# Gathering six of the last eight mode rows before the last weights are in, in a fused linear-attention and spectral-mixing kernel

## The chip, the cores and the metric

One Trainium2 chip, and of its cores one. The metric is the device time of one execution in microseconds (us). Before the change it is 421.44 us, the median of three runs that lie between 421.43 and 421.51.

## The reference

Eight batches, eight heads, 576 positions, head size 64, so 512 channels. A linear attention with the feature map phi(x) = elu(x) + 1 gives x; a real Fourier transform along the positions keeps 64 modes; each mode multiplies its own complex 512 x 512 weight; the inverse transform gives y, and a channel product with a ReLU closes it.

```
kv = einsum('bhsd,bhse->bhde', phi(k), v);  num = einsum('bhsd,bhde->bhse', phi(q), kv)
x  = num / (den + 1e-06)                    # rearranged to (8, 576, 512)
X  = rfft(x, axis=1)[:, :64]
Yr = Xr @ w_r - Xi @ w_i;   Yi = Xr @ w_i + Xi @ w_r        # per mode, 512 x 512 each
u  = x + irfft(Yr + 1j * Yi, n=576, axis=1)
out = u + maximum(u @ w_ch, 0.0)
```

The weights of the 64 modes are 128 MB in float32, by far the most of what is read.

## The kernel before

**Order of the work.** First comes the attention and the forward transform, while inputs and the first weights arrive. Then a loop over 32 pairs of modes (`mode_pair`, lines 462 to 483): each pair's 2 MB of weights (in bf16) come by two transfers on the GpSimd queue (POOL), TensorE (PE) multiplies them, and small transposing products (`picks`) put the mode rows, 16 columns for each mode (real and imaginary part of eight batches), into a PSUM tile `yt_ps`. Between the pairs, work on earlier modes is dealt out from a list (`work_slot`). PE is given filler products (`keep_warm`, line 416), as many as the table `FILL` of line 535 says for the pair. `pin` keeps an instruction in program order on its engine.

**The last pair** is mode 62 and mode 63 (`last_pair`, lines 487 to 519). Their weights come as eight transfers (`w_load_last`, line 122): three of 512 KB, and the fourth cut into five pieces, three of 128 KB and two of 64 KB (`PIECES`), so that PE can follow each piece as it arrives (line 513). The rows of the last eight modes (56 to 63) are gathered in `Y8`: modes 56 to 62 at line 506, mode 63 at line 519.

**The late rows.** With `Y8` complete, lines 921 to 950 turn it: four transposes give the rows y (128 rows, 8 modes x 16), eight products of 128 x 256 with the channel weights give z, the same rows after the channel product. Both go into one tile `last` of 128 partitions x 2 x 512 (f16). Two transfers, one on the SyncE queue (SP) and one on POOL (lines 946 to 950, 256 KB each), then spread these rows into `YZ_all`, which holds for every batch and each of two halves of the partitions the 64 rows of modes 32 to 63: every fourth row is one of the last eight modes.

**The end.** The output is 36 tiles of 128 positions x 512, taken as 18 pairs. For each pair, `channels` (line 792) puts the channel product's early part into a PSUM accumulator, `add_inverse(n, 1)` (line 755) adds the part from z, a ReLU on ScalarE (ACT) follows, `add_inverse(n, 0)` adds the part from y, and VectorE (DVE) adds x; then SP stores. Batches 0 and 1, which are pairs 0 to 3, read `last` directly with 128 rows (`lead_sb`); all others read `YZ_all` with 64 rows (`inv2_sb`), tile 0 of a pair from partitions 0 to 63 and tile 1 from 64 to 127. For pairs 0 to 3 the order is written out by hand, tile by tile (lines 982 to 988): for each of seven tiles, in turn, PE adds the y part, makes the sums of one tile two pairs ahead (`sums_of`: channels, z part, ReLU), and DVE adds and SP stores 256 KB (`add_one`, line 960). The sums ahead are those of pairs 2, 3 and 4, a tile at a time. From pair 5 on whole pairs are handled (`rectified`, `finish`, lines 806 and 829), with one DVE addition of 128 x 1024 and one store of 512 KB.

```
    singles = [(n, i) for n in range(4) for i in range(2)][1:]
    ahead = [(n, i) for n in (2, 3, 4) for i in range(2)]
    for n, i in singles:
        add_inverse(n, 0, (i,))
        if ahead:
            sums_of(*ahead.pop(0))
        add_one(n, i)
```

The functions that the change touches:

Of the kernel before, what the change touches and what calls it, by code (L numbers as in the profile page):

```python
# [10 lines left out]
F32 = mybir.dt.float32  # L11
F16 = mybir.dt.float16
# [31 lines left out]
def kernel(  # L44
# [10 lines left out]
    nc = tc.nc  # L55

    B, H, S, Dh = q.shape
    D = H * Dh
    NM = moe_w_r.shape[0]
    NHP = H // 2  # L60
    NDC = D // 128
# [5 lines left out]
    NL = 8  # L67
    NE = NM - NL
    NF = NM // 2

    fwd_np, inv_np, pick_np = _dft_consts(S, NM)
    id16_dr = nc.inline_tensor(np.eye(128, dtype=np.float16), name="ident16")
# [8 lines left out]
    id16 = const.tile([128, 128], F16, name="id16")  # L81
    fwd_sb = const.tile([128, 5, 2 * NM], F16, name="fwd_sb")
    pick_sb = const.tile([128, 32], F16, name="pick_sb")
    wch16 = const.tile([128, NDC, D], F16, name="wch16")
# [21 lines left out]
    pin = tc.keep_in_program_order  # L106
# [15 lines left out]
    def w_load_last(pool, tag: str, bufs: int):  # L122
        w_in[LAST] = pool.tile([128, NDW, D], BF16, tag=tag, bufs=bufs, name=f"w{LAST}")
        for g in range(2):
            for half in range(2):
                rows_in = (moe_w_r, moe_w_i)[half][NM - 2 + g].rearrange("(p dc) e -> p dc e", dc=NDL)
                for dcs in PIECES if (g, half) == (1, 1) else (slice(0, NDL),):
                    dst = w_in[LAST][half::2, g * NDL + dcs.start : g * NDL + dcs.stop]
                    pin(nc.gpsimd.dma_start(out=dst, in_=rows_in[:, dcs, :]))

    w_in: dict[int, object] = {}


    W_PRE = 3
# [16 lines left out]
    def rows_of(jj: int, base: int = 0):  # L151

        if jj < NJJ:
            return slice(base + jj, base + 512, NJJ)
        return slice(512, S) if base == 0 else slice(0, base)
# [268 lines left out]
    def work_slot(p: int, name: str):  # L424
        for _ in range(slots.get((p, name), 0)):
            if work:
                work.pop(0)()
# [59 lines left out]
    def last_pair():  # L487
        xl = ystage.tile([128, NDL, 2 * B], BF16, name="xl")
        for h in range(2):
            src = xt_v[:, (2 * h + 1) * NDC : (2 * h + 2) * NDC, :, :, LAST]  # L490
            pin(
                nc.vector.tensor_copy(
                    out=xl[:, h * NDC : h * NDC + NDC], in_=src.rearrange("p c t b -> p c (t b)")
                )
            )
        w = w_get(LAST)
        kk = NM - 2
        work_slot(LAST, "start")
        P = psW.tile([128, D], F32, tag="P", bufs=2, name=f"P{kk}")
        for dc in range(NDL):  # L500
            n = 32 if dc < NDC else 2 * B
            product(P, xt_cols(dc, kk, n), n, w, dc, NDL)
        st = evacuate(kk, P)
        work_slot(LAST, "mid")
        picks(kk, st, 1)
        pin(nc.vector.tensor_copy(out=Y8[:, :, 0 : NL - 1, :], in_=yt_ps[:, :, 0 : NL - 1, :]))
        keep_warm(3)
        y_last = psW.tile([128, NDC, 2 * B], F32, tag="P", bufs=2, name="y_last")
        for piece in PIECES:
            for dc in range(piece.start, piece.stop):  # L510
                for ec in range(NDC):
                    pin(
                        nc.tensor.matmul(
                            y_last[:, ec, :], w[:, NDL + dc, ec * 128 : ec * 128 + 128], xl[:, dc, :],
                            start=(dc == 0 and ec == 0), stop=(dc == NDL - 1), skip_group_check=True,
                        )
                    )
            keep_warm(WARM[piece.stop])
        nc.vector.tensor_copy(out=Y8[:, :, NL - 1, :], in_=y_last)

# [9 lines left out]
    psW = tc.alloc_tile_pool(name="psW", bufs=1, space=PSUM, side="left")  # L530
# [1 line left out]


    n_early = n_keep + n_pre
    FILL = {**{p: 7 for p in range(5, 16)}, **{p: 7 for p in range(18, 27)}, 27: 7, 28: 10, 29: 12, 30: 10}
    ystage = ctx.enter_context(tc.tile_pool(name="ystage", bufs=1, side="right"))
    inv_sb = ystage.tile([2 * NM, S], F16, name="inv_sb")
    inv2_sb = ystage.tile([128, S], F16, name="inv2_sb")
# [1 line left out]
    lead_sb = [ystage.tile([128, S], F16, name=f"lead{b}_sb") for b in range(N_LEAD)]  # L540
    nc.sync.dma_start(out=inv_sb, in_=inv_dr.ap())
    YE_T = ystage.tile([128, NDC, NF, 2 * B], F16, name="YE_T")
    YL = [ystage.tile([128, NDC // 2, 2, 2 * NL, NF // NL, B], F16, name="YL0")]
    Y8 = ystage.tile([128, NDC, NL, 2 * B], F16, name="Y8")

    def late_modes(g: int, ps):

# [19 lines left out]
    yt_ps = None  # L567
# [9 lines left out]
    sW = ctx.enter_context(tc.tile_pool(name="sW", bufs=1))  # L577
# [4 lines left out]
    YZ_all = sW.tile([128, B, 2, D], F16, tag="YZ", bufs=1, name="YZ_all")  # L582
# [24 lines left out]
    last_ps = []  # L607
# [67 lines left out]
    x16w, xTw = {}, {}  # L675
# [79 lines left out]
    def add_inverse(n: int, half: int, tiles_of=(0, 1)):  # L755

        def mm(i, orow, l, r):
            on_bank(
                n, {i},
                nc.tensor.matmul(  # L760
                    accs[n][orow, i], l, r, start=False, stop=True, skip_group_check=True
                ),
            )

        for i in tiles_of:
            for b, jj, orow in parts_of(pairs[n][i]):
                sel_rows = rows_of(jj, BASE[b % 2])
                if n < 2 * N_LEAD:
                    mm(i, orow, lead_sb[b][:, sel_rows], last[:, half, :])
                else:  # L770
                    g = HALVES[i]
                    mm(i, orow, inv2_sb[g, sel_rows], YZ[b][g, half, :])
# [19 lines left out]
    def channels(n: int, tiles_of=(0, 1)):  # L792
        if n not in accs:
            accs[n] = acc_pools[n % 4 // 2].tile([128, 2, D], F32, tag="acc", bufs=2, name=f"acc{n}")
        for i in tiles_of:
            t = pairs[n][i]
            for cols, src in e0_parts(t):
                on_bank(
                    n, {i},
                    nc.tensor.matmul(  # L800
                        accs[n][:, i, cols], id16, src, start=(cols.start == 0), stop=False,
                        skip_group_check=True,
                    ),
                )
# [103 lines left out]
    for p in range(n_early, LAST):  # L908
        mode_pair(p)
    assert not work  # L910
    psB.release()
    acc_pools.append(
        tc.alloc_tile_pool(name="psT0", bufs=1, space=PSUM, side="right", reuse_waits="tile")
# [2 lines left out]
    for n in range(N_PRE):  # L916
# [1 line left out]
    last_pair()  # L918


    last = sW.tile([128, 2, D], F16, tag="rows", bufs=1, name="last")
    z1_ps = psW.tile([128, NDC, 8, 2 * B], F32, tag="yt", bufs=1, name="z1l")
    y_ps = [
        psW.tile([128, NDC, 128], F16, tag="P", bufs=2, name=f"ypl{h}")[:, 0 : NDC // 2] for h in range(2)
    ]
    y0 = psW.tile([128, D], F32, tag="P", bufs=2, name="y0l")
    last_ps.append(z1_ps.rearrange("p c m n -> p (c m n)"))
    rows = [Y8[:, ec].rearrange("p m n -> p (m n)") for ec in range(NDC)]
    hw = D // 2
    COLS = [slice(h * hw, h * hw + hw) for h in range(2)]  # L930
    for ec in range(NDC):
        pin(nc.tensor.transpose(y_ps[ec // 2][:, ec % 2, :], rows[ec], id16))
    pin(nc.scalar.copy(out=last[:, 0, COLS[0]], in_=y_ps[0].rearrange("p c r -> p (c r)")))
    pin(nc.vector.tensor_copy(out=last[:, 0, COLS[1]], in_=y_ps[1].rearrange("p c r -> p (c r)")))
    for h in range(2):
        for ec in range(NDC):
            pin(
                nc.tensor.matmul(
                    last_ps[h][:, 0:hw], rows[ec], wch16[:, ec, COLS[h]],
                    start=(ec == 0), stop=(ec == NDC - 1),  # L940
                )
            )
        pin(nc.scalar.copy(out=last[:, 1, COLS[h]], in_=last_ps[h][:, 0:hw]))
    pin(nc.tensor.matmul(y0, lead_sb[0][:, rows_of(0)], last[:, 0, :]))
    pin(nc.vector.tensor_tensor(out=x_of(0), in0=y0, in1=x_of(0), op=ALU.add))
    for h, eng in enumerate((nc.sync, nc.gpsimd)):
        eng.dma_start(
            out=YZ_all[64 * h : 64 * h + 64 : NF // NL].rearrange("r b z d -> r b (z d)"),
            in_=last.rearrange("p z d -> p (z d)"),
        )  # L950
    psW.release()
    acc_pools.append(
        tc.alloc_tile_pool(name="psT1", bufs=1, space=PSUM, side="left", reuse_waits="tile")
# [2 lines left out]
    def relu(n: int, i: int):  # L956
        a = accs[n][:, i]
        on_bank(n, {i}, nc.scalar.activation(out=a, in_=a, func=AF.Relu))
# [3 lines left out]
        on_bank(n, {i}, nc.vector.tensor_tensor(out=x_of(t), in0=accs[n][:, i], in1=x_of(t), op=ALU.add))  # L962
        store(t, 1)

    def sums_of(n: int, i: int):
        channels(n, (i,))
        add_inverse(n, 1, (i,))
        relu(n, i)

    add_inverse(0, 1, (1, 0))  # L970
    on_bank(
# [2 lines left out]
            out=x_of(0), in0=accs[0][:, 0], scalar=0.0, in1=x_of(0), op0=ALU.max, op1=ALU.add  # L974
# [5 lines left out]
        add_inverse(1, 1, (i,))  # L980
        relu(1, i)
    singles = [(n, i) for n in range(4) for i in range(2)][1:]
    ahead = [(n, i) for n in (2, 3, 4) for i in range(2)]
    for n, i in singles:
        add_inverse(n, 0, (i,))
        if ahead:
            sums_of(*ahead.pop(0))
        add_one(n, i)
    for n in range(5, len(pairs)):
        channels(n)  # L990
# [34 lines left out]
```

## Time and profile before

| what | value |
|---|---|
| time, median of three runs | 421.44 us (421.43 to 421.51) |
| span of the profiled execution, first to last instruction | 419.4 us |
| time less span | 2.0 us |
| PE busy | 317.2 us (76%) |
| DVE busy | 231.3 us (55%) |
| ACT busy | 154.2 us (37%) |
| POOL busy | 57.4 us (14%) |
| read from HBM, written to it | 163.93 MB, 9.44 MB |

Times inside the execution are microseconds from the start of its span. A line of a timeline gives the start, the busy time, the engine, the line of the code, the operation, the tile written and the tile read, how many such instructions are merged in it, and in brackets the idle time of the engine before it with what ended that. A line of issued transfers gives the queue, how many there were, the size of each and the median time from issue to landing. A line of a table by stages gives a stretch of time, each engine's busy time in it, PE's granted clock, the share of the time in which the 16 DMA engines were busy, and the rate.

### The profile page before, as it was taken

What the parts mean: (1) busy time and instruction counts of PE and PEld (TensorE: products, weight loads), DVE (VectorE), ACT (ScalarE), POOL (GpSimd) and SP (SyncE); (2) the same over time, 40 slices, a digit from 0 to 9 for tenths busy, and PEclk for the clock granted to TensorE, in tenths of its full rate; (3) what the DMA queues carried; (4) which work ended last, traced back from release to release, by engine and by line L of the source; (5) the groups of instructions that cost most, each with busy time, mean ns of one, the idle gap of its engine ahead of it and who ended that gap; (6) DMA issues with size and microseconds to landing.
All of it is one profiled execution on the core that took longest, in us unless ns stands there. A gap on an engine that the chain in (4) does not pass through costs nothing.

```text
span 419.4 us, 7466 instructions
## 1 busy us (share of the span) xinstructions
PE 317.2 (76%) x3143; PEld 164.4 (39%) x3143; DVE 231.3 (55%) x509; ACT 154.2 (37%) x253; POOL 57.4 (14%) x100
## 2 busy tenths in 40 slices
PE   0369998999617875676767686988798877998993
PEld 0257776877301332222222233433343332453421
DVE  4588899785314563463645353464456443522794
ACT  4677798854201011000000233334253432330783
POOL 4222224210011211111111111111111111130000
PEclk9999999579855658665655599899899997899998
DMA  8999999999999999999999999999999999998698
GB/s 217 211 212 216 210 222 203 228 206 223 217 223 208 218 220 209 220 217 212 220 214 213 223 213 214 223 210 216 220 209 219 217 214 219 216 209 166 235 391 328
DMA packets 17073, 93.17 MB, mean 222 GB/s; under 512 B 2112, under 2 KB 3024, under 8 KB 12880
## 3 DMA queue, kind: packets, MB, share of 16 engines
q0 software_dynamic: 12496, 81.48, 93.4%
q1 hardware_dynamic: 4544, 11.22, 7.2%
q8 instruction: 24, 0.39, 0.3%
q14 instruction: 9, 0.07, 0.0%
HBM read 163.93 MB, written 9.44 MB: 413 GB/s over the span
## 4 chain that ended last, share of the span: by engine, by line
DMA 64%; PE 23%; DVE 4%; POOL 3%; ACT 3%; issue 2%; DVEq 0%; ACTq 0%; POOLq 0%
DMA w<-in_moe_w_i_dram 53%; DMA pick_sb<-row_pick 8%; PE P L432 6%; DMA k<-in_k_dram 3%; PE acc L760 3%; PE kvp L257 3%; PE acc L800 2%; POOL w L117 2%; PE z L726 1%; DVE x L293 1%; ACT ke L208 1%; PE xf L355 1%; PE zl L419 1%; PE qTp L237 1%; PE num L163 1%
## 5 line engine op out<-in xcount | busy, mean ns | idle before, releaser
L432 PE MATMUL P<-w,xz 128*32 128x512 bf16 x496 | 42.6, 475 | 37.6 <-DMA w<-in_moe_w_i_dram 35.4
L419 PE MATMUL zl<-wch,id 128*128 128x512 f16 x185 | 58.2, 466 | 0.0
L449 ACT CAST ys<-P 128x512 f16<-128x512 f32 x15 | 8.8, 586 | 132.4 <-PE P L432 132.4
L117 POOL DMA_DIRECT2D w<-in_moe_w_r_dram x31 | 17.3, 559 | 246.4 <-PE P L432 211.8
L447 DVE CAST ys<-P 128x512 f16<-128x512 f32 x17 | 11.8, 692 | 51.0 <-PE P L432 51.0
L706 PE MATMUL eps<-wch,xTw 128*128 128x512 f16 x144 | 39.3, 399 | 0.0
L432 PEld LDWEIGHTS <-xz 128*32 128x32 bf16 x496 | 12.6, 108 | 63.3 <-DMA w<-in_moe_w_i_dram 40.3
L163 PEld LDWEIGHTS <-qT 64*128 64x128 f16 (+1 forms) x640 | 22.6, 122 | 29.6 <-issue 15.6
L689 ACT CAST x16w<-x_main 128x512 f16<-128x512 f32 x32 | 19.8, 618 | 37.8 <-DVE x_main L687 37.8
L687 DVE TENSOR_TENSOR x_main<-ya,x_main 128x512 f32<-128x512 f32 x32 | 22.0, 689 | 16.5 <-PE ya L683 16.3
L257 PE MATMUL kvp<-vpad,ke 32*128 32x130 f16 x576 | 24.3, 263 | 8.9 <-ACT qT L244 6.1
L442 DVE COPY xz<-xt_c 64x256 bf16<-64x256 bf16 x62 | 23.0, 371 | 10.9 <-PE P L432 10.0
L419 PEld LDWEIGHTS <-id 128*128 128x128 f16 x185 | 18.9, 112 | 25.6 <-issue 14.3
L714 ACT CAST E<-eps 128x512 f16<-128x512 f32 (+1 forms) x40 | 21.2, 540 | 17.7 <-PE eps L706 17.7
L257 PEld LDWEIGHTS <-ke 32*128 32x128 f16 x576 | 22.3, 116 | 10.6 <-issue 8.6
L163 PE MATMUL nw<-kv_sb,qT 64*128 64x65 f16 (+1 forms) x320 | 18.2, 231 | 9.8 <-DVE x_tail L650 4.7
L237 PE MATMUL qTp<-id,qe 128*128 128x128 f16 x144 | 15.1, 289 | 10.6 <-DVE qe L221 9.5
L293 DVE TENSOR_TENSOR x<-num,rd 128x512 f16<-128x512 f32 x32 | 22.1, 692 | 1.1
L650 DVE TENSOR_TENSOR x_main<-nw,rd 128x256 f32<-128x256 f32 x32 | 11.2, 416 | 18.8 <-PE nw L163 18.8
L455 PE MATMUL yt<-pick_sb,ys 128*128 128x32 f16 (+1 forms) x128 | 8.8, 185 | 16.7 <-DMA pick_sb<-row_pick 9.4
L698 DVE COPY xTw<-xTp 128x512 f16<-128x512 f16 x36 | 15.0, 416 | 10.3 <-PE xTp L696 10.3
L208 ACT ACTIVATE qe<-q 128x1152 f16<-128x1152 f16 (+1 forms) x16 | 17.9, 1157 | 7.2 <-DMA q<-in_q_dram 7.1
(118 smaller groups left out, 507.5 us busy)
## 6 DMA issues: line engine op xcount, KB each, us to landing
w<-in_moe_w_r_dram POOLq DMA_DIRECT2D x31, 1024.0 KB, 13.2
w<-in_moe_w_i_dram POOLq DMA_DIRECT2D x31, 1024.0 KB, 17.5
out_dram<-x_main SPq DMA_DIRECT2D x12, 512.0 KB, 3.6
k<-in_k_dram POOLq DMA_DIRECT2D x8, 576.0 KB, 12.9
v<-in_v_dram POOLq DMA_DIRECT2D x8, 576.0 KB, 14.3
q<-in_q_dram POOLq DMA_DIRECT2D x7, 576.0 KB, 12.6
out_dram<-x_main SPq DMA_DIRECT2D x8, 256.0 KB, 4.0
q<-in_q_dram SPq DMA_DIRECT2D x2, 576.0 KB, 4.5
```

Source lines behind the costliest of these rows:

```text
L117: nc.gpsimd.dma_start(out=w_in[p][half::2], in_=two.rearrange("g (r dc) e -> (g r) dc e", dc=NDW))
L163: mm = nc.tensor.matmul(num[hpo][orow, c0 : c0 + 65], qT[rows, hpp, h2, cols], kv_sb[rows, hpp, h2, :])
L208: pin(nc.scalar.activation(out=ev[:, c], in_=heads(nm, b, c), func=AF.Exp))
L257: nc.tensor.matmul(kv_ps[:, h2, 0:130], phi["k", b][r0 : r0 + 32, j // NJ, j % NJ].rearrange("p o d -> p (o d)"), vp[r0 : r0 + 32, :, j, 0 ...
L293: nc.vector.tensor_tensor(out=dst.rearrange("p (o c d) -> p o c d", o=2, c=4), in0=nv[:, :, :, 0:64], in1=rden.unsqueeze(3).broadcast_to([ ...
L419: pin(nc.tensor.matmul(last_ps[0], id16, wch16[:, 0, :]))
L432: nc.tensor.matmul(P[c : c + n, :], x, w[:, dc, :], start=(dc < NDC), stop=(dc >= n_dc - NDC), tile_position=(0, c), skip_group_check=True,)
L442: pin(nc.vector.tensor_copy(out=xz[p % 2][HALVES[h], :, h, :], in_=src))
L687: pin(nc.vector.tensor_tensor(out=x, in0=acc, in1=x, op=ALU.add))
L689: pin(nc.scalar.copy(out=x16w[t], in_=x))
L706: nc.tensor.matmul(e_ps, xT[:, c, :], wch16[:, c, :], start=(c == 0), stop=(c == NDC - 1))
L714: pin(nc.scalar.copy(out=dst, in_=e_ps[:, cols]))
```

## The change

It has three parts. First, the rows of modes 56 to 61 (`NA` = 6 modes, `RA` = 96 rows) are turned ahead, at the start of the last pair (`ahead_rows`), from a `Y8` whose last two modes are zero: one copy on DVE, four transposes and four products on PE, two copies on ACT into a tile `ahead`. Eight of the ten fillers of pair 30 go. Two transfers, one on SP and one on POOL, spread these rows into `YZ_all` (`ahead_gathers`); a dependency written by hand makes them wait for the last weight piece but two. Second, at the old place, only the 32 rows of modes 62 and 63 are spread, by four transfers, all on POOL: z for the two halves, then y for the two halves. `last` becomes two tiles, but it is still made in full, and pairs 0 to 3 read all of it as before. Third, the sums of pair 4 are made together for its two tiles, where before they came one tile at a time.

```
+    NA = NL - 2
+    RA = 2 * B * NA
...
-                    pin(nc.gpsimd.dma_start(out=dst, in_=rows_in[:, dcs, :]))
+                    pieces.append(pin(nc.gpsimd.dma_start(out=dst, in_=rows_in[:, dcs, :])))
...
         kk = NM - 2
+        ahead_rows()
         work_slot(LAST, "start")
...
-        pin(nc.vector.tensor_copy(out=Y8[:, :, 0 : NL - 1, :], in_=yt_ps[:, :, 0 : NL - 1, :]))
+        pin(nc.vector.tensor_copy(out=Y8[:, :, NA, :], in_=yt_ps[:, :, NA, :]))
+        ahead_gathers()
         keep_warm(3)
...
-    FILL = {..., 27: 7, 28: 10, 29: 12, 30: 10}
+    FILL = {..., 27: 7, 28: 10, 29: 12, 30: 2}
...
+    nc.vector.memset(Y8[:, :, NA:NL, :], 0.0)
...
+    def ahead_rows():
+        pin(nc.vector.tensor_copy(out=Y8[:, :, 0:NA, :], in_=yt_ps[:, :, 0:NA, :]))
+        ya_ps = psW.tile([128, NDC, 128], F16, tag="P", bufs=2, name="ya_ps")
+        za_ps = psW.tile([128, D], F32, tag="P", bufs=2, name="za_ps")
+        for ec in range(NDC):
+            pin(nc.tensor.transpose(ya_ps[:, ec, :], rows[ec], id16))
+        for ec in range(NDC):
+            pin(nc.tensor.matmul(za_ps, rows[ec], wch16[:, ec, :], start=(ec == 0), stop=(ec == NDC - 1)))
+        pin(nc.scalar.copy(out=ahead[0:RA, 0, :], in_=ya_ps[0:RA].rearrange("p c r -> p (c r)")))
+        pin(nc.scalar.copy(out=ahead[0:RA, 1, :], in_=za_ps[0:RA]))
+
+    def late_at(h: int, r0: int, n: int):
+        at = 64 * h + r0 // B * (NF // NL)
+        return YZ_all[at : 64 * h + 64 : NF // NL][0 : n // B]
+
+    def ahead_gathers():
+        for h, eng in enumerate((nc.sync, nc.gpsimd)):
+            g = eng.dma_start(
+                out=late_at(h, 0, RA).rearrange("r b z d -> r b (z d)"),
+                in_=ahead[0:RA].rearrange("p z d -> p (z d)"),
+            )
+            pin(g)
+            tc.add_manual_dep(g.ins, pieces[-3].ins.name, ...)
...
-    for h, eng in enumerate((nc.sync, nc.gpsimd)):
-        eng.dma_start(
-            out=YZ_all[64 * h : 64 * h + 64 : NF // NL].rearrange("r b z d -> r b (z d)"),
-            in_=last.rearrange("p z d -> p (z d)"),
-        )
+    for z in (1, 0):
+        for h in range(2):
+            nc.gpsimd.dma_start(out=late_at(h, RA, 128 - RA)[:, :, z, :], in_=last[z][RA:128])
...
-    def sums_of(n: int, i: int):
-        channels(n, (i,))
-        add_inverse(n, 1, (i,))
-        relu(n, i)
+    def sums_of(n: int, tiles_of):
+        channels(n, tiles_of)
+        add_inverse(n, 1, tiles_of)
+        for i in tiles_of:
+            relu(n, i)
...
-    ahead = [(n, i) for n in (2, 3, 4) for i in range(2)]
+    soon = [(n, (i,)) for n in (2, 3) for i in range(2)] + [(4, (0, 1))]
```

More of the change, by code (lines that the diff above doesn't have):

```diff
@@ L128, in w_load_last @@
                     dst = w_in[LAST][half::2, g * NDL + dcs.start : g * NDL + dcs.stop]
-                    pin(nc.gpsimd.dma_start(out=dst, in_=rows_in[:, dcs, :]))
+                    pieces.append(pin(nc.gpsimd.dma_start(out=dst, in_=rows_in[:, dcs, :])))
     w_in: dict[int, object] = {}
+    pieces: list = []
     W_PRE = 3
@@ L534 @@
     n_early = n_keep + n_pre
-    FILL = {**{p: 7 for p in range(5, 16)}, **{p: 7 for p in range(18, 27)}, 27: 7, 28: 10, 29: 12, 30: 10}
+    FILL = {**{p: 7 for p in range(5, 16)}, **{p: 7 for p in range(18, 27)}, 27: 7, 28: 10, 29: 12, 30: 2}
     ystage = ctx.enter_context(tc.tile_pool(name="ystage", bufs=1, side="right"))
@@ L544 @@
     Y8 = ystage.tile([128, NDC, NL, 2 * B], F16, name="Y8")
+    nc.vector.memset(Y8[:, :, NA:NL, :], 0.0)
+    rows = [Y8[:, ec].rearrange("p m n -> p (m n)") for ec in range(NDC)]
     def late_modes(g: int, ps):
@@ L768, in add_inverse @@
                 if n < 2 * N_LEAD:
-                    mm(i, orow, lead_sb[b][:, sel_rows], last[:, half, :])
+                    mm(i, orow, lead_sb[b][:, sel_rows], last[half])
                 else:
@@ L910 @@
     assert not work
+    ahead = sW.tile([128, 2, D], F16, tag="rows", bufs=1, name="rows_ahead")
+    def ahead_rows():
[5 more added lines that the diff above has]
+        for ec in range(NDC):
+            pin(
+                nc.tensor.matmul(
+                    za_ps, rows[ec], wch16[:, ec, :], start=(ec == 0), stop=(ec == NDC - 1)
+                )
+            )
+        pin(nc.scalar.copy(out=ahead[0:RA, 0, :], in_=ya_ps[0:RA].rearrange("p c r -> p (c r)")))
[8 more added lines that the diff above has]
+                in_=ahead[0:RA].rearrange("p z d -> p (z d)"),
+            )
+            pin(g)
+            tc.add_manual_dep(
+                g.ins,
+                pieces[-3].ins.name,
+                mybir.DependencyInfo(mybir.DependencyClass.Sync, mybir.DependencyReason.DATA),
+                reason="behind most of the last weights",
+            )
     psB.release()
@@ L918 @@
     last_pair()
-    last = sW.tile([128, 2, D], F16, tag="rows", bufs=1, name="last")
+    last = [
+        sW.tile([128, D], F16, tag="x16w", bufs=2, name="last_y"),
+        sW.tile([128, NDC, 128], F16, tag="xTw", bufs=2, name="last_z").rearrange("p c r -> p (c r)"),
+    ]
     z1_ps = psW.tile([128, NDC, 8, 2 * B], F32, tag="yt", bufs=1, name="z1l")
@@ L927 @@
     last_ps.append(z1_ps.rearrange("p c m n -> p (c m n)"))
-    rows = [Y8[:, ec].rearrange("p m n -> p (m n)") for ec in range(NDC)]
     hw = D // 2
@@ L932 @@
         pin(nc.tensor.transpose(y_ps[ec // 2][:, ec % 2, :], rows[ec], id16))
-    pin(nc.scalar.copy(out=last[:, 0, COLS[0]], in_=y_ps[0].rearrange("p c r -> p (c r)")))
-    pin(nc.vector.tensor_copy(out=last[:, 0, COLS[1]], in_=y_ps[1].rearrange("p c r -> p (c r)")))
+    pin(nc.scalar.copy(out=last[0][:, COLS[0]], in_=y_ps[0].rearrange("p c r -> p (c r)")))
+    pin(nc.vector.tensor_copy(out=last[0][:, COLS[1]], in_=y_ps[1].rearrange("p c r -> p (c r)")))
     for h in range(2):
@@ L942 @@
             )
-        pin(nc.scalar.copy(out=last[:, 1, COLS[h]], in_=last_ps[h][:, 0:hw]))
-    pin(nc.tensor.matmul(y0, lead_sb[0][:, rows_of(0)], last[:, 0, :]))
+        pin(nc.scalar.copy(out=last[1][:, COLS[h]], in_=last_ps[h][:, 0:hw]))
+    pin(nc.tensor.matmul(y0, lead_sb[0][:, rows_of(0)], last[0]))
     pin(nc.vector.tensor_tensor(out=x_of(0), in0=y0, in1=x_of(0), op=ALU.add))
-    for h, eng in enumerate((nc.sync, nc.gpsimd)):
-        eng.dma_start(
-            out=YZ_all[64 * h : 64 * h + 64 : NF // NL].rearrange("r b z d -> r b (z d)"),
-            in_=last.rearrange("p z d -> p (z d)"),
-        )
+    for z in (1, 0):
+        for h in range(2):
+            nc.gpsimd.dma_start(out=late_at(h, RA, 128 - RA)[:, :, z, :], in_=last[z][RA:128])
     psW.release()
@@ L982 @@
     singles = [(n, i) for n in range(4) for i in range(2)][1:]
-    ahead = [(n, i) for n in (2, 3, 4) for i in range(2)]
+    soon = [(n, (i,)) for n in (2, 3) for i in range(2)] + [(4, (0, 1))]
     for n, i in singles:
         add_inverse(n, 0, (i,))
-        if ahead:
-            sums_of(*ahead.pop(0))
+        if soon:
+            sums_of(*soon.pop(0))
         add_one(n, i)
```

## The prediction

> **What bounds the kernel now.** I read the page first, for where transfers bound and where not; then the table by stages of the end; then the lines of PE and DVE around pair 4; last the landings.
>
> ```profile
> DMA  8999999999999999999999999999999999998698
> ...
> DMA 64%; PE 23%; DVE 4%; POOL 3%; ACT 3%; issue 2%; DVEq 0%; ACTq 0%; POOLq 0%
> ```
>
> The DMA engines are nearly full for 36 slices of 10.5 us, and the chain lies 64% on them: until the last weights are in (388 us), nothing that the other engines save counts. The dips to 8 and 6 and what follows are the end, and the whole change works there. By stages:
>
> ```profile
> core 0: us, PE busy (x) PEld busy (x) DVE busy (x) ACT busy (x) POOL busy (x), PEclk, DMA share, GB/s
> 388.00:391.50 3.50, 3.15 (x24) 1.81 (x24) 1.84 (x4) 1.97 (x5) 0.57 (x1) 1.00 0.02 5
> 391.50:394.00 2.50, 2.50 (x13) 1.29 (x12) 2.36 (x5) 2.42 (x5) 0.00 (x0) 1.00 0.99 279
> 394.00:398.50 4.50, 4.50 (x23) 1.20 (x21) 3.72 (x6) 3.39 (x8) 0.00 (x0) 1.00 1.05 393
> 398.50:399.25 0.75, 0.75 (x10) 0.31 (x7) 0.75 (x1) 0.50 (x2) 0.00 (x0) 1.00 0.65 249
> 399.25:417.50 18.25, 13.12 (x72) 3.27 (x72) 14.68 (x13) 11.78 (x22) 0.00 (x0) 0.98 1.01 401
> ```
>
> 388 to 391.5 is the turning of the late rows, with the DMA engines empty (0.02). 391.5 to 394 holds the two gathers and the first stores, at a low rate (279 GB/s). Then the stores run at 393 to 401 GB/s. The line to look at is 398.5 to 399.25: a **hole**, share 0.65. The single stores have drained before pair 4's store of 512 KB arrives. After the hole the engines are full to the end: 14 stores of 0.524 MB at 401 GB/s are 18.3 us, and 399.25 + 18.3 = 417.5. So the end is the start of pair 4's store plus 18.3 us. The landings say the same: pair 4's store (issued at 398.34) waits for nobody, the last (414.13) waits 1.0 us:
>
> ```profile
> out_dram<-x_main SPq DMA_DIRECT2D x1, 512.0 KB, 3.1
> ...
> out_dram<-x_main SPq DMA_DIRECT2D x1, 512.0 KB, 4.1
> ```
>
> DVE gives a pair every 1.22 us, the transfers take one every 18.3 / 14 = 1.31 us: DVE paces no store behind pair 4's. What sets pair 4's store is DVE's addition at 397.09, and what delays that is here:
>
> ```profile
> 393.65 0.59 PE L760 MATMUL acc<-last,lead_sb 128*128 128x512 f16 x2
> 394.09 0.38 PE L800 MATMUL acc<-E,id 128*128 128x512 f16 x1
> 394.40 0.40 PE L760 MATMUL acc<-YZ_all,inv_sb 64*128 64x512 f16 x1
> 394.73 0.41 PE L760 MATMUL acc<-last,lead_sb 128*128 128x512 f16 x1
> 394.98 0.38 PE L800 MATMUL acc<-E,id 128*128 128x512 f16 x1
> 395.29 0.40 PE L760 MATMUL acc<-YZ_all,inv_sb 64*128 64x512 f16 x1
> 395.62 0.41 PE L760 MATMUL acc<-last,lead_sb 128*128 128x512 f16 x1
> 395.87 0.59 PE L800 MATMUL acc<-E,id 128*128 128x512 f16 x2
> 396.40 0.62 PE L760 MATMUL acc<-YZ_all,inv_sb 64*128 64x512 f16 x4
> ...
> 391.70 3.28 DVE L962 TENSOR_TENSOR x_main<-acc,x_main 128x512 f32<-128x512 f32 x5
> 395.18 0.69 DVE L962 TENSOR_TENSOR x_main<-acc,x_main 128x512 f32<-128x512 f32 x1 [0.20 <-PE acc L760]
> 396.07 0.69 DVE L962 TENSOR_TENSOR x_main<-acc,x_main 128x512 f32<-128x512 f32 x1 [0.20 <-PE acc L760]
> 397.09 3.76 DVE L834 TENSOR_TENSOR x_main<-acc,x_main 128x1024 f32<-128x1024 f32 x3 [0.32 <-PE acc L760]
> ```
>
> Products of 128 rows follow each other 0.22 us apart; from a product of 128 rows to one of 64 it takes 0.31 (394.09 to 394.40), back 0.33 or 0.25. Pair 4's sums, a tile at a time, make the change twice, and DVE, dense before, idles 0.20 + 0.20 + 0.32 = 0.72 us.
>
> **The change part by part.** *The rows turned ahead.* Added: a DVE copy of 128 x 384 (between the rows of 128 x 64, 0.22, and 128 x 448, 0.62: 0.55), four transposes and four products of 128 x 512 (as the late turning: 0.06 and 0.22 apart, 1.1 us together), two ACT copies of 0.59 at most. Removed: eight fillers at 0.22, 1.72 us. In order of time: pair 30's picks end at 380.2, two fillers run to 380.7, the copy ends at 380.85, PE turns until 382.0. Before, the next work began at 382.21: nothing changes. ACT has no other work there. The cover: PE waits for the first piece until 386.14 and again until 386.67 and 387.26; 0.3 us of lateness is absorbed. Past that it would cost one for one. The copy at line 506 shrinks from 0.62 to about 0.2, off the path. The memset is 128 columns in a DMA-bound stretch: nothing.
>
> *The two early transfers.* 393 KB. They wait for the piece that released PE at 387.26. Queued behind the wait: on SP nothing until the first store (391.59), on POOL only the late rows (390.49). Issue costs 0.66 (SP) and 0.57 (POOL); the old gathers landed 3.7 and 4.3 us after issue, so these land by 391 to 392, mostly in the empty stretch. The last two pieces (64 KB each) are issued long before and land by 387.9. Cost nothing. Gain: three quarters of the gathers' bytes leave the stretch 391.5 to 394. But what that frees, the hole swallows: single stores land earlier, and pair 4's store comes no sooner. The only way to gain is through those engines that were still at old stores in the hole: between 0 and 0.65 x 0.75 = 0.5 us. I take 0, since pair 4's store landed in the shortest time, and keep 0.5 for the range.
>
> *The late rows by four transfers.* Before, z and y of tile 0 left on SP at 390.21 (landed 393.9) and those of tile 1 on POOL at 390.49 (landed 394.8); PE read them at 394.40 and 395.29, each 0.31 after the product before, the plain change of rows: neither waited. Now POOL issues z for both halves at 390.49 and 391.06, y at 391.63 and 392.20. What a transfer of 32 KB takes from POOL, no row shows. Above: the 256 KB one, 4.3. Below: its first packets move past 392.4 (1.9 after issue), its data take 1.4 us, the rest 0.9 is receipt; with an eighth of the data, 1.9 + 0.2 + 0.9 = 3.0. I take the middle, 3.65, since the only row is eight times as large and the stores still compete: the second z lands at 394.7 (394.1 to 395.4), the second y at 395.85 (395.2 to 396.5).
>
> *Pair 4's sums together.* PE now: y part of the tile before at 393.87, two channel products 394.09 and 394.31, both z parts at 394.62 (the two halves of rows run side by side, as the four at 396.40 do), back at 394.95 and 395.17 for pair 3's two tiles, pair 5's channels at 395.38 and 395.60, its z at 395.91, pair 4's y at 396.15 (its second ReLU ends at 395.05 + 0.49 + 0.58 = 396.12), out at 396.55. DVE: pair 3's first tile 0.20 **later** (394.95 + 0.43 = 395.38), its second at 396.03, pair 4 at 396.73 in place of 397.09: **0.36 earlier**. Pair 5 keeps it: its second ReLU ends 0.5 earlier. Against this stands the wait for the second z, 394.7 - 394.62 = 0.1 (0 to 0.75); y, wanted at 396.15, is in time except at the upper end, where PE is itself 0.75 late.
>
> **Sum.** 0.36 - 0.1 = 0.26, rounded to 0.3 us off pair 4's store, and as much off the end: a span of 419.1. The time is 2.0 us above the span now (421.44 against 419.4), so 421.1 us. Own range: 421.44 - 0.36 - 0.5 = 420.6 to 421.44 - 0.36 + 0.75 = 421.8.
>
> **A rule against it.** The trace's own price is 3.7 to 4.3 us for 256 KB. The Trainium skill (DMA: Bandwidth & Descriptors, Rules for kernel authors) says to coalesce small transfers into one large one, since under 64 KB one mostly pays overhead, and that splitting by partition halves brings nothing. Its Anatomy section fits 2.0 us plus bytes / 436e3; by that estimate 256 KB would take 2.6, which the trace exceeds by 1.1 to 1.7, and 32 KB would take 2.1, landing the second z at 393.2 with no wait and a time of 421.1 all the same. The same page's section on the semaphore's 16 says that a transfer uses the largest number of engines up to 16 that divides both sides' slowest dimension: with 4 partitions written it would be 4 engines. No row here shows that; it would push z to the upper end.
>
> **Rivals.**
> *The late rows land late* (against: a row eight times as large needs 4.3; for: four issues of 0.57 in a line on POOL, among stores). At 4.3 each, pair 4's z waits 0.75, net + 0.4: 421.8. It turns slower than before from a second z past 395.0 on.
> *Pair 4's z sums wait for all four transfers*, because they cross POOL's queue as one, or because the wait is not told apart by z and y. Then PE stands until the second y, 395.2 to 396.5: a wait of 0.6 to 1.9 less 0.36, 421.7 to 423.0, likeliest 422.3. It passes the 0.2% from a landing at 395.85 on.
> *The gathers' DMA time counts after all*: if the engine that ends last was never idle in the hole, its whole queue moves up. 0.393 MB at 279 GB/s is 1.4 us: 420.0. Against it: share 0.65 in the hole, 3.1 us for pair 4's store.
> *It moves nothing*: the sums' order shifts waits only, 421.4.
>
> **How the numbers follow.** 0.2% (0.84 us) is about what a measurement of this kernel tells from no change. Forecast 0.60, late rows 0.15, all four 0.07, DMA time counts 0.12, nothing 0.06. Faster by over 0.2% (under 420.6) is the DMA rival and a hair of the forecast: 0.13. Slower (over 422.28) is half of the all-four case and a tail of the late one: 0.07. The rest, 0.80, is within. The range 420.4 to 421.9 leaves out the outer parts of two rivals.
>
> **What would show it.** Right: pair 4's two z products side by side near 394.6, DVE's first 128 x 1024 addition near 396.8, a wider hole at 398, stores full to the end. Wrong: an idle PE between pair 4's channels and its z ended by a transfer; a last store that lands sooner than pair 4's store moved; y_last's products later than 387.93.

## The result and the profile after

The changed kernel takes 420.94 us (median of 22 executions, 420.62 to 422.26), the kernel before on the same chip 421.57 us (421.22 to 422.12). The ratio is 0.9986, 95% interval 0.998 to 0.9993: 0.59 us less (0.30 to 0.84), where the forecast was 0.3 and the range 420.4 to 421.9. The gain is clear of noise, and its interval reaches just to the 0.2% that the prediction took as the least that a measurement tells.

In the profiled executions the last weights land at 387.88 us before and 388.20 after, and everything behind them is late by as much. So the ends are compared here from a common origin, the start of the late rows' four transposes (388.51 before, 388.83 after); the chain from the last weights to it is the same in both. The changed kernel, PE's and DVE's lines around pair 4:

```profile
388.83 0.40 PE L978 MATMUL ypl<-id,Y 128*128 128x128 f16 x4
...
394.40 0.59 PE L807 MATMUL acc<-E,id 128*128 128x512 f16 x2
394.93 0.41 PE L767 MATMUL acc<-YZ_all,inv_sb 64*128 64x512 f16 x2
395.27 0.62 PE L767 MATMUL acc<-last_y,lead_sb 128*128 128x512 f16 x2
395.73 0.59 PE L807 MATMUL acc<-E,id 128*128 128x512 f16 x2
396.26 0.62 PE L767 MATMUL acc<-YZ_all,inv_sb 64*128 64x512 f16 x4
...
392.02 3.28 DVE L1006 TENSOR_TENSOR x_main<-acc,x_main 128x512 f32<-128x512 f32 x5
395.72 1.29 DVE L1006 TENSOR_TENSOR x_main<-acc,x_main 128x512 f32<-128x512 f32 x2 [0.42 <-PE acc L767]
396.95 2.51 DVE L841 TENSOR_TENSOR x_main<-acc,x_main 128x1024 f32<-128x1024 f32 x2
```

Both z products of pair 4 stand in one line at 394.93, 0.31 after the last channel product: nothing but the change of rows, no wait for a transfer. DVE idles 0.42 us once in place of 0.72 in three pieces, and its first addition of 128 x 1024 starts 396.95 - 388.83 = 8.12 us after the origin, before 397.09 - 388.51 = 8.58: 0.46 sooner. The last store lands 29.23 us after the origin, before 29.75: 0.52 sooner.

The transfers of the changed kernel, the late rows and the first and last 512 KB store, by window of issue (the last column is the time to landing), and its table by stages:

```profile
YZ_all<-last_z POOLq DMA_DIRECT2D x1, 32.0 KB, 2.8
...
YZ_all<-last_z POOLq DMA_DIRECT2D x1, 32.0 KB, 3.0
...
YZ_all<-last_y POOLq DMA_DIRECT2D x1, 32.0 KB, 3.3
...
out_dram<-x_main SPq DMA_DIRECT2D x1, 512.0 KB, 2.6
...
out_dram<-x_main SPq DMA_DIRECT2D x1, 512.0 KB, 4.1
```

```profile
388.00:391.50 3.50, 3.17 (x27) 1.95 (x26) 1.52 (x4) 1.65 (x5) 1.33 (x3) 1.00 0.39 116
391.50:394.00 2.50, 2.48 (x13) 1.20 (x12) 2.36 (x5) 2.42 (x6) 1.66 (x3) 1.00 0.54 165
394.00:398.50 4.50, 4.50 (x25) 1.46 (x23) 4.02 (x7) 3.75 (x8) 0.00 (x0) 1.00 1.01 373
398.50:399.25 0.75, 0.75 (x9) 0.23 (x6) 0.75 (x1) 0.50 (x2) 0.00 (x0) 1.00 0.84 322
399.25:417.50 18.25, 12.98 (x72) 3.26 (x70) 14.56 (x13) 11.65 (x22) 0.00 (x0) 0.95 1.01 398
```

The early rows now move in the stretch that was empty (share 0.39 where it was 0.02), 391.5 to 394 is half empty (0.54), and from 399.25 on the stores fill the engines as before (398 GB/s).

### The profile page after: what moved, and what is told of

Its sections match the earlier page's. It is cut to its first block, busy times and chain, and to the rows that moved or that the text cites. A ratio compares the mean times of both kernels' runs of the same rounds, so it can differ in the third digit from the quotient of the medians.

```text
span 419.2 us, 7479 instructions
## 1 busy us (share of the span) xinstructions
PE 313.1 (75%) x3143; PEld 162.6 (39%) x3143; DVE 231.2 (55%) x511; ACT 155.1 (37%) x255; POOL 59.1 (14%) x104
## 4 chain that ended last, share of the span: by engine, by line
DMA 60%; PE 24%; DVE 6%; issue 3%; ACT 3%; POOL 3%; DVEq 0%; ACTq 0%; POOLq 0%
DMA w<-in_moe_w_i_dram 48%; DMA pick_sb<-row_pick 8%; PE P L435 7%; DMA k<-in_k_dram 3%; PE acc L767 3%; PE kvp L260 2%; PE zl L422 2%; PE acc L807 2%; PE eps L713 2%; DVE x L296 1%; POOL w L119 1%; PE z L733 1%; ACT ke L211 1%; PE yb L752 1%; ACT qT L247 1%
## 5 line engine op out<-in xcount | busy, mean ns | idle before, releaser
L422 PE MATMUL zl<-wch,id 128*128 128x512 f16 x177 | 55.9, 466 | 0.0
L240 PE MATMUL qTp<-id,qe 128*128 128x128 f16 x144 | 14.1, 276 | 11.5 <-DVE qe L224 9.5
```

Source lines behind the costliest of these rows:

```text
L422: pin(nc.tensor.matmul(last_ps[0], id16, wch16[:, 0, :]))
```

## The experiments

In the table, "pair 4" is the time from the origin to DVE's first addition of 128 x 1024, "last" that to the last landing, both from the run's one profiled execution. "Before" is the kernel before on the same chip. How far such times repeat: the changed kernel, fill_10 and no_wait agree within 0.01 and 0.03 us, the two runs with the sums alone within 0.03 and 0.13, so steps of 0.1 to 0.2 in the column "last" stand on little. What happens ahead of the origin, these columns leave out.

| run | pair 4 | last | time | before | ratio (95%) |
|---|---|---|---|---|---|
| kernel before | 8.58 | 29.75 | 421.57 | | |
| changed kernel | 8.12 | 29.23 | 420.94 | 421.57 | 0.9986 (0.998 to 0.9993) |
| sums_only | 8.17 | 29.40 | 420.92 | 421.22 | 0.9996 (0.9987 to 1.0004) |
| gathers_only | 8.58 | 29.60 | 421.30 | 421.22 | 1.0007 (0.9998 to 1.0015) |
| z_last | 8.49 | 29.62 | 420.94 | 421.22 | 0.9994 (0.9986 to 1.0003) |
| fill_10 | 8.12 | 29.25 | 421.11 | 421.22 | 1.0 (0.9992 to 1.0009) |
| no_wait | 8.12 | 29.24 | 420.98 | 421.50 | 0.9987 (0.9978 to 0.9996) |
| singles_9 | tile by tile | 29.15 | 420.98 | 421.50 | 0.9987 (0.9978 to 0.9996) |
| after_again | 9.34 | 30.50 | 420.88 | 421.50 | 0.9986 (0.9977 to 0.9995) |
| sums_again | 8.19 | 29.53 | 421.11 | 421.50 | 0.999 (0.9981 to 0.9999) |
| traffic_after | 8.12 | 29.68 | 421.20 | 421.19 | 1.0 (0.9991 to 1.0009) |
| traffic | 8.38 | 29.71 | 421.24 | 421.19 | 0.9999 (0.999 to 1.0007) |
| traffic_late | 8.44 | 30.16 | 421.77 | 421.59 | 1.0005 (0.9996 to 1.0014) |

**sums_only**: the third part of the change alone, on the kernel before.

```
-    ahead = [(n, i) for n in (2, 3, 4) for i in range(2)]
+    soon = [(n, (i,)) for n in (2, 3) for i in range(2)] + [(4, (0, 1))]
```

> The kernel before with the third part of the change alone: pair 4's sums made together; the late rows are gathered as before, by two transfers of 256 KB on SP and POOL. As origin in each run serves the start of the late rows' transposes; from it to DVE's first addition of 128 x 1024 it is 8.58 us before and 8.12 after the change. Theory A (the whole gain is the order of the sums): 8.1 plus the wait for the second z, which lands 4.3 us after its issue, that is 6.3 after the origin, where PE wants it 6.1 after: 8.1 to 8.3, and a time 0.2 to 0.45 us under before, at most 0.25 above the changed kernel. Theory B (the gain is the DMA time of the gathers, moved out of the stretch of the first stores): no gain, the time of before within 0.2 us, although DVE's addition comes earlier; the last landing is as late as before.

PE's and DVE's lines around pair 4, and the stage of the hole:

```profile
394.12 0.59 PE L800 MATMUL acc<-E,id 128*128 128x512 f16 x2
394.64 0.45 PE L760 MATMUL acc<-YZ_all,inv_sb 64*128 64x512 f16 x2
...
395.47 1.29 DVE L962 TENSOR_TENSOR x_main<-acc,x_main 128x512 f32<-128x512 f32 x2 [0.46 <-PE acc L760]
396.70 2.51 DVE L834 TENSOR_TENSOR x_main<-acc,x_main 128x1024 f32<-128x1024 f32 x2
```

```profile
398.50:399.25 0.75, 0.75 (x7) 0.26 (x8) 0.72 (x2) 0.50 (x2) 0.00 (x0) 1.00 1.02 402
```

Pair 4 at 8.17, the last landing 29.40: 0.41 of the 0.46 us on DVE and 0.35 of the 0.52 us at the end come from one line of order. The hole is closed (1.02). The second z product starts 0.07 late, the wait for the old gather. Theory A's reading of the profile holds; the time fell by 0.17 us by the ratio (0.30 between the medians) with an interval that holds no change.

**gathers_only**: the changed kernel without that line.

```
-    soon = [(n, (i,)) for n in (2, 3) for i in range(2)] + [(4, (0, 1))]
+    soon = [(n, (i,)) for n in (2, 3, 4) for i in range(2)]
```

> The changed kernel with pair 4's sums one tile at a time again: early gathers and four late transfers stay. Theory A: 8.58 us from origin to DVE's first addition of 128 x 1024, and the time of before, within 0.15 us. Theory B (DMA time): most of the gain stays, 0.4 us or more under before, with a last landing that comes sooner after pair 4's store than the 19.9 us of before. Both theories together would show half.

Pair 4 is back at 8.58, and the time is that of before. DVE's lines and the stages around the hole:

```profile
395.40 0.69 DVE L1006 TENSOR_TENSOR x_main<-acc,x_main 128x512 f32<-128x512 f32 x1 [0.20 <-PE acc L767]
396.30 0.69 DVE L1006 TENSOR_TENSOR x_main<-acc,x_main 128x512 f32<-128x512 f32 x1 [0.20 <-PE acc L767]
397.31 2.51 DVE L841 TENSOR_TENSOR x_main<-acc,x_main 128x1024 f32<-128x1024 f32 x2 [0.33 <-PE acc L767]
```

```profile
398.00:398.50 0.50, 0.50 (x5) 0.01 (x1) 0.50 (x1) 0.47 (x2) 0.00 (x0) 1.00 1.03 397
398.50:399.25 0.75, 0.75 (x9) 0.41 (x8) 0.69 (x2) 0.73 (x2) 0.00 (x0) 1.00 0.40 153
399.25:402.00 2.75, 2.75 (x20) 0.72 (x16) 2.67 (x3) 2.23 (x5) 0.00 (x0) 1.00 0.96 383
```

The three idle pieces of 0.20, 0.20 and 0.33 are back, and the hole is deeper than before the change (0.40 against 0.65): what the gathers no longer take, pair 4's late store leaves unused. Only 0.15 us of it reaches the last landing, and none the time (1.0007). Its interval lies wholly above that of the changed kernel (0.9998 against 0.9993), so the time too needs the line of order.

**z_last**: the late transfers as y, y, z, z.

```
-    for z in (1, 0):
+    for z in (0, 1):
```

> The changed kernel with the four late transfers in the other order, y for both halves, then z. It prices the rival that the late rows arrive late: the second z now takes the place of the second y, which landed 7.1 us after the origin, where PE wants z 6.1 after. If the landing counts one for one: an idle PE of 0.8 to 1.0 us ended by a transfer, 9.0 us to DVE's first addition of 128 x 1024, and 0.8 to 1.0 us above the changed kernel, slower than before by about 0.4. If the DMA engines or DVE swallow a late pair 4, the time stays within 0.2 us of the changed kernel.

The y rows are ready sooner than z, so the first transfer went out at 390.09, 1.43 us after the origin and not 1.97; the second z landed 6.47 after the origin, not 7.1. PE:

```profile
394.24 0.59 PE L807 MATMUL acc<-E,id 128*128 128x512 f16 x2
394.76 0.78 PE L767 MATMUL acc<-YZ_all,inv_sb 64*128 64x512 f16 x2
395.47 0.62 PE L767 MATMUL acc<-last_y,lead_sb 128*128 128x512 f16 x2
```

The two z products, 0.41 together when both rows are there, take 0.78. That is 0.40 between their starts, 0.37 on pair 4 and 0.39 at the last landing: a late z row costs one for one, with a dose that was half of the one expected. By the time alone (0.9994) it could not have been told.

**fill_10**: ten fillers behind pair 30 again.

```
-    FILL = {..., 30: 2}
+    FILL = {..., 30: 10}
```

> The changed kernel with ten fillers behind pair 30 as before, in place of two: the turning ahead is then wholly added on PE, eight fillers of 0.216 us, 1.7 us, ahead of the last pair. It tells what PE's cover is worth. By the prediction 0.3 us is absorbed; by the waits seen in the changed kernel's last pieces (0.32, 0.16 and 0.13 us) 0.6 us is. So the late rows' transposes start 1.1 to 1.4 us later after the last weights' landing, and the time is 1.1 to 1.4 us above the changed kernel. If PE were not the pace there (the weights were), nothing changes.

The median is level with before, and the ratio about 0.6 us above the changed kernel's, with executions from 420.42 to 422.31 us. In the profiled one (422.31 us) the origin lies 2.3 us behind the last weights, 0.6 in the changed kernel: 1.7 later, more than the 1.1 to 1.4 expected, and by another cause:

```profile
376.00:380.00 4.00, 1.84 (x25) 0.57 (x23) 0.86 (x3) 0.00 (x0) 0.53 (x1) 1.00 1.05 219
380.00:384.00 4.00, 4.00 (x18) 1.56 (x16) 0.72 (x3) 0.00 (x0) 0.00 (x0) 0.57 1.00 200
...
379.98 4.00 PE L422 MATMUL zl<-wch,id 128*128 128x512 f16 x10
```

The granted clock (third column from the right) is 0.57: the ten fillers took 4.00 us where they took 2.32 before. The 1.68 us between the two are all that this execution lost, so it doesn't price the eight fillers: at the full clock, by this estimate, they would have cost it nothing. The profiles of sums_again and traffic_late have the same half clock in the same place and ten fillers, but nothing turned ahead; there the origin lies 1.15 and 1.20 us behind the last weights, with the same lead of PE (in all three, pair 30's picks end 7.7 us ahead of the last weights). The 1.1 us to this run's 2.30 are the turning ahead, when PE has no lead left to cover it. That the fastest executions had lead enough for the fillers is an inference from their times; none of them was profiled.

**no_wait**: the changed kernel without `tc.add_manual_dep(...)`.

> The changed kernel without the dependency written by hand: the two early transfers start as soon as their rows are made and pair 1's products have read the old rows, about 1.5 us sooner. If they take the DMA engines from the last weight pieces: 393 KB at some 400 GB/s is up to 1.0 us that the last piece lands later, and the time is 0.3 to 1.0 us above the changed kernel. If the last pieces, which leave engines idle (about 60 GB/s in their last stretch), run beside them: within 0.2 us. In neither case does the stretch from the origin (start of the late rows' transposes) to DVE's first addition of 128 x 1024 change from 8.12 us.

The early transfers were issued at 383.03 (POOL) and 384.86 (SP), against 388.30 and 387.80: 5.3 and 2.9 us sooner, not the 1.5 expected. The last weights landed at 388.05, inside the 387.8 to 388.2 of all other profiles, and time and last landing are those of the changed kernel. The wait is worth nothing that shows.

**singles_9**: pair 4 finished tile by tile.

```
+        if n == 5:
+            for i in range(2):
+                add_inverse(4, 0, (i,))
+                add_one(4, i)
+        else:
             finish(n - 1)
```

> The changed kernel with pair 4 finished tile by tile too: two DVE additions of 128 x 512 and two stores of 256 KB in place of one of each. It tests the hole. Pair 4's first store then starts 0.5 us sooner (a DVE addition of 0.65 in place of 1.23), its second 0.1 us later. If the end is set by when the DMA engines are filled again, it comes earlier by what the hole leaves idle, 0.16 of 0.75 us, 0.1 us, and up to 0.3 if the stores that lag are fed sooner. If DVE paced the stores, the end comes 0.1 us later.

Its stages:

```profile
398.00:398.50 0.50, 0.50 (x5) 0.31 (x4) 0.47 (x2) 0.50 (x2) 0.00 (x0) 1.00 1.03 389
398.50:399.25 0.75, 0.75 (x9) 0.25 (x8) 0.75 (x1) 0.50 (x2) 0.00 (x0) 1.00 1.00 374
```

The first store of pair 4 leaves 0.57 us sooner, the hole is closed (1.00), and the last landing comes 0.08 us sooner, as small as expected; the time doesn't tell it from the changed kernel.

**after_again** and **sums_again**: the changed kernel and sums_only side by side on one chip.

> The changed kernel itself, on the chip of the other runs of this set, so that they can be compared with it: 0.3 to 0.6 us under before, and 8.12 us from the origin to DVE's first addition of 128 x 1024 again.

> The kernel before with the sums of pair 4 together alone, beside the changed kernel on the same chip: what the early gathers add to the order of the sums. In the profiles so far the last landing is 29.75 us behind the origin before, 29.40 with the sums alone, 29.60 with the gathers alone, 29.23 with both. If these add up, this kernel is 0.15 to 0.2 us above the changed one; if the gathers are worth nothing, level; if they cost on the way to the last weights, below it.

420.88 against 421.11 us: the early gathers add 0.2 us to the order of the sums, as the last landings have it (29.23 against 29.40 and 29.53); by the times alone, whose intervals overlap, this could not be told. Against before, 0.6 and 0.4 us, with both intervals below 1. The profile of after_again misses its expectation (9.34): this execution, 422.04 us, had the clock at half just where the late rows are turned, which the last section comes to.

**traffic_after, traffic, traffic_late**: two more transfers of 128 KB each on POOL, read by nobody, behind the late rows of the changed kernel and of sums_only.

```
+    for z in range(2):
+        nc.gpsimd.dma_start(out=spare[z], in_=last[z])
```

> The changed kernel with two more transfers of 128 KB behind the late rows on POOL, from the two tiles of late rows into spare tiles that nobody reads: 0.39 MB of gather traffic beside the stores, where the changed kernel has 0.13, and the kernel with the sums alone 0.52 (its last landing: 29.40 to 29.53 us behind the origin, against 29.23). Hole theory: pair 4's addition stays at 8.12, the share of the DMA engines between the single stores and pair 4's rises towards 1, and the last landing comes at 29.25 to 29.45, not 0.65 later, which is what 0.26 MB take at 0.4 MB per us. If DMA time counts fully, 29.8 to 29.9.

> The kernel with pair 4's sums together and the old gathers, with the same two more transfers of 128 KB on POOL: 0.79 MB of gather traffic beside the stores. With 0.52 MB no hole was left (share 1.02). Hole theory: now every byte more counts, so the last landing comes 0.6 to 0.7 us later than with the sums alone, 30.0 to 30.2, and the time rises by as much, while DVE's first addition of 128 x 1024 stays within 0.1 us of 8.17. If the engines still swallow it, 29.4 to 29.6. The second z lands later only if the new transfers, issued behind it, slow it.

> As the run with 0.79 MB of gather traffic, where one of the two added transfers went out 0.7 us ahead of the gather and so ran before the first store's data: here both are held behind the gather on POOL, so that all of the added 0.26 MB meets the stores. With no hole left (share 1.02 with the sums alone) it should cost its whole DMA time: 0.26 MB at 0.4 MB per us, 0.65 us, so a last landing at 30.0 to 30.2 us behind the origin, where the sums alone have 29.40 and 29.53, and a time 0.5 to 0.7 us above theirs against the same before. If half or less of it shows (up to 29.85), the engines still have room that the share does not show.

traffic_after: pair 4 unmoved at 8.12, the share in the hole 1.01, the last landing at 29.68, 0.45 later. Of 0.65 us of transfers the hole took 0.2 by this profile. The time (1.0 against 0.9986) puts the cost at 0.6, with intervals wide enough for both. The expectation of at most 0.2 fell; the full price fell by the profile, not by the time. traffic: one spare transfer went out at 389.94, ahead of the gather and of all stores, so only half of the dose met them, and 0.2 to 0.3 us showed at the last landing. The second z waited 0.29 us, so pair 4 came at 8.38, outside the 0.1 us around 8.17 that was expected. traffic_late, with both held behind the gather: 30.16, later by 0.76 and 0.63 than the two profiles with the sums alone, the full price and more; its second z also waited 0.35. The share between the single stores and pair 4's (399.24 to 399.99 here) is 1.05, so no idle stretch explains the delay; the time is 0.4 to 0.6 us above that of the sums alone by the ratios.

## Why the prediction was right

*The mechanism and the sign* were right: two changes of rows fewer, DVE's pair 4 sooner, the stores full to the end behind it. sums_only and gathers_only show it from both sides. The size was less well met: the gain is about twice the forecast. That 420.94 lies so near to 421.1 is in part luck, since the kernel before read 421.57 here and 421.44 when the forecast was made.

*The signs.* Side by side products, DVE's earlier addition and full engines to the end came as named (394.61 and 396.63 in the clock of before, which is 0.32 sooner). The wider hole did not: the DMA share in it rose from 0.65 to 0.84. The gathers do empty it (0.40 in gathers_only), but pair 4's earlier store fills more of it. And the last store gained 0.52 us where pair 4's addition gained 0.46, a sign that the prediction had put down as wrong; the 0.06 is within what two profiles differ by.

*Pair 4's sums together*, forecast 0.36, measured 0.46. Pair 3's first tile stood where it was put (395.40 in the clock of before; forecast 395.38), its second too. But the additions behind them start 0.61 and 0.62 apart (1.29 us for two), not the 0.65 and 0.70 of the forecast: DVE overlaps the start of one with the end of the other, also from 512 to 1024 columns. One reading in the prediction is off and enters no sum: the way back from 64 to 128 rows takes 0.33; the 0.25 beside it lies between two products of 128 rows (394.73 to 394.98).

*The wait for the second z*, taken as 0.1 (0 to 0.75), was 0. It landed 3.0 us after its issue, the lower bound, and 0.49 before PE wanted it; the first took 2.8, below it. The bound was made with the 0.9 us between the old gather's last data and its landing, under full engines; here they were half empty, which may be why. In four other runs with early gathers the first late row took only 2.10 to 2.11 us (no_wait, singles_9, fill_10, after_again). z_last confirms the price that a late row would have had. With both terms as measured the sum is 0.46; the last landing moved by 0.52 and the time by 0.59 (0.30 to 0.84).

*What the early gathers free, the hole swallows*: taken as 0 of 0 to 0.5 us; it is about 0.2 (0.17 and 0.30 in the landings, 0.23 between two medians whose intervals overlap). The reason given was only half of it. The hole takes about 0.2 us (traffic_after). The rest was never in the stores' way, as the kernel before shows around its first store:

```profile
390.63:391.50 0.87, 0.85 (x5) 0.32 (x3) 0.73 (x2) 0.85 (x2) 0.42 (x1) 1.00 0.00 0
391.50:392.43 0.93, 0.93 (x6) 0.51 (x5) 0.79 (x3) 0.93 (x3) 0.00 (x0) 1.00 0.93 209
392.43:393.50 1.07, 1.07 (x7) 0.52 (x6) 1.07 (x2) 0.99 (x3) 0.00 (x0) 1.00 1.08 337
```

and the changed kernel in the same places, 0.3 us later:

```profile
391.95:392.70 0.75, 0.75 (x6) 0.34 (x4) 0.68 (x2) 0.75 (x3) 0.75 (x3) 1.00 0.29 66
392.70:393.50 0.80, 0.80 (x5) 0.41 (x4) 0.80 (x3) 0.78 (x2) 0.46 (x1) 1.00 0.94 320
```

Without the big gathers the engines fill at 392.7, when the first store's data start; that is 392.4 in the clock of before, and there the SP gather had run from 391.5 to 392.4. So about 0.9 us of the old gathers' time lay in a stretch that nobody wanted. The rival that all the moved DMA time counts (420.0) fell by this, not by the hole alone.

*The rows turned ahead and the two early transfers* cost nothing that the aligned profile or the median shows, as forecast, and the hand-written wait covers nothing (no_wait). But the early transfer on POOL landed 5.1 us after its issue, at 393.39 and not by 391 to 392; it was without a price, since pair 4's z read its rows at 394.93. Rare long executions may be its price (last section). The cover, put at 0.3 us, is larger: in sums_again PE lost 1.68 us on the fillers (4.00 in place of 2.32) and the origin only 0.53, an estimate of 1.15 us absorbed. The Trainium skill's rule against small transfers (DMA: Bandwidth & Descriptors, Rules for kernel authors) stands beside four transfers of 32 KB at 2.8 to 3.3 us, where the fit of its Anatomy section gives an estimate of 2.1. They are mostly fixed time, as it says: 256 KB took 3.7 and 4.3. They are harmless here, since nothing waited for them. What the same page says of the number of engines (section on the semaphore's 16) is near to a row: while the late rows run alone, 391.95 to 392.70, the share is 0.29, on the mean 4.6 of 16 engines, where its rule gives 4 for one such transfer. A share doesn't count engines, so the row agrees and doesn't prove it.

## What to carry to other kernels

Where an engine's idle time comes in equal small pieces, look for an order of the instructions that pays a fixed cost (here the change between products of 128 and of 64 rows, 0.31 to 0.33 us from start to start in place of 0.22) once for several tiles. Before moving transfers out of a busy stretch, look at when the stretch's other transfers can start: bytes that run before that, or that end in a later gap, are free already. Differences of 0.1 to 0.5 us in a kernel of 421 are read from profiles aligned at a common event, and only then compared with times.

## What the runs showed of the hardware

PE's clock halves for single windows also at this end of the kernel, and in one profile that cost more than the change gains. In after_again the granted clock is 0.50 from 388.83 to 392.24, 3.41 us. The profile of after_again, by stages, and of the changed kernel's first profile in the same stretch:

```profile
385.00:388.75 3.75, 2.95 (x44) 1.54 (x41) 0.45 (x2) 0.00 (x0) 0.63 (x1) 1.00 0.38 66
388.75:392.25 3.50, 3.47 (x16) 1.86 (x15) 0.98 (x2) 1.54 (x4) 0.80 (x2) 0.51 0.40 117
```

```profile
385.00:388.75 3.75, 3.55 (x45) 1.75 (x44) 0.90 (x3) 0.00 (x0) 0.45 (x1) 1.00 0.46 80
388.75:392.25 3.50, 3.16 (x21) 1.93 (x22) 1.93 (x5) 2.40 (x6) 1.63 (x4) 1.00 0.42 121
```

Granted 0.51, the late rows' products took nearly twice as long (1.05 us for four in place of 0.60), and pair 4 came 1.2 us later (9.34). The Trainium skill (TensorE: Matmul & The Clock Gate, Part 1) has the clock halve after an idle window of about 3.4 us; here PE was busy 2.95 of the 3.75 us ahead of it (3.55 in the profile without it), so it was less busy, and not idle.

Such windows of 3.41 us stand in three more of the thirteen profiles, all of kernels with ten fillers behind pair 30: from 380.24 in fill_10, from 380.60 in sums_again, from 380.39 in traffic_late. There they slow the fillers (from sums_again, as in fill_10):

```profile
380.22 4.00 PE L419 MATMUL zl<-wch,id 128*128 128x512 f16 x10
```

In the two kernels with nothing turned ahead the origin came 0.5 to 0.6 us further behind the last weights than in the profiles without such a window there (0.62).

Of 88 executions of kernels with two fillers behind pair 30, seven lay 1.1 us or more above their kernel's median; of 170 of the kernel before and of kernels with its ten fillers and nothing turned ahead, none did. So the change, or rather its first two parts (two of the seven are of gathers_only, none of the runs with the sums alone), brings rare long executions, about 0.1 us on the mean. One of the seven was profiled; whether the other six have its cause, and whether the eight fillers taken out bring it on, stays open.
